# A two-layer FFT-filter and dense kernel: filter rows of two groups fetched earlier, and one piece of an inverse transform moved behind the first transposes

## The chip, the cores and the metric

One core of one Trainium2 chip. The metric is device microseconds (us) of one execution. The kernel before takes 1016.25 us (median of three runs, 1016.15 to 1018.78). Engines: PE is the matmul engine (PEld its weight loads), DVE the vector engine, ACT the activation engine, POOL the general engine, which here mostly issues DMAs, and SP a queue that issues DMAs.

## The reference, cut to what matters

```python
def _A_ref(x, w_r, w_i):                       # spectral layer, x is 1 x 2048 x 1024 bf16
    X = rfft2(x.astype(float32), axes=(-2, -1))
    X = X * (w_r + 1j * w_i)                   # filter, 2048 x 513
    return irfft2(X, s=(S, D), axes=(-2, -1)).astype(bfloat16)

def _B_ref(x, w1, b1, w2):                     # dense layer, 1024 -> 3584 -> 1024
    h = einsum("bsd,df->bsf", x, w1) + b1
    ...                                        # act = Mish(h)
    return einsum("bsf,fd->bsd", act, w2)

x = A_x
x = x + _A_ref(_layernorm(x), A_w_r, A_w_i)
x = x + _B_ref(_layernorm(x), B_w1, B_b1, B_w2)
x = x + _A_ref(_layernorm(x), A_w_r, A_w_i)
x = x + _B_ref(_layernorm(x), B_w1, B_b1, B_w2)
```

## The kernel before

The FFTs are products with DFT matrices on PE. A spectral layer first transforms all of the input with one set of matrices (the first step; in the first layer these are scaled matrices, the tile MN). The rest is cut into 8 groups of frequencies. Each group goes through a second step, a filter multiplication, a third step and two inverse steps, and its result goes through memory (`u_scratch`) into a buffer `UT`. When all 8 are there, the last inverse step (`i4`) makes the output. The groups overlap in a fixed order; in the code `stage, g, h` are the step, the group and its half.

In the first layer the filter must be put into the order of the groups. Its rows come from memory into a ring of two buffers (`WR`), four small matmuls (`filter_bins`) and three engines of copies turn them into filter tiles:

```python
def load_w(self, g):
    if self.li == 0:
        self.load_wr(self.WR[g % 2], g)        # two DMAs: real rows, imaginary rows
        return
    ...

self.s1(li)                                    # first step, frees MN
...
self.UT = self.alloc("UT", o["UT"], [P, P])    # lies over MN
...
for stage, g, h in self.order_A():
    if stage == 2:
        s2(g, h)
        if li == 0 and h == 0:
            filter_bins(g)
            if g < 6:
                load_w(g + 2)                  # waits until the copies of g have read WR
    elif stage == 3:
        s3(g, h)
        if h:
            if g < 6:
                load_tabs(g + 2)               # forward table
            ...
    elif stage == 4:
        i1(g, h)
        if h and g < 6:
            load_btabs(g + 2)                  # inverse table, tile name c_bt
    else:
        i2(g, h)
        u_turn(g, h)
```

All these loads stand in POOL's one queue, in program order (in the trace of before, group 6's two row transfers at 67.45 and 68.16, the table after them at 68.89).

The dense layer starts (its "head") with what the spectral layer left to do for the first rows: `i4` for four blocks of rows, then the layer norm of the first two, their transposes on PE, and the first dense matmuls. The other 12 blocks of rows of `i4` are cut into pieces, called by `rest(bank)`, that are strewn among the first dense matmuls:

```python
        self.root(0, 2)
        rest(0)                                # 15 matmuls of 96 columns, one wide ACT evacuation
        rest(3)                                # 15 more, the piece that the change moves
        for j in range(2):
            xn[j] = self.apply(j)              # DVE: normalise
        for j in range(2):
            transposed(0, j, xn[j])            # PE: 8 transposes each, DVE copies them out
        self.warm(ACT.Mish)                    # ACT: table load
        at_tiles(0)
        ...
        for fg in range(4):
            mm1(0, fg, 0, ...)                 # first dense matmuls
            rest(3)
```

## Time and profile before

The profiled execution spans 1013.1 us. Of the page, besides what the prediction shows, the chain of work that ended last (the first line by engine, the second by line of code; each figure is a share of the span) is what tells how little can be reached here:

```profile
PE 87%; DMA 4%; SPq 3%; DVE 2%; ACT 2%; issue 1%; POOL 0%; ACTq 0%; DVEq 0%
PE PS L1067 38%; PE PS L1050 38%; SPq L249 3%; PE PS L771 2%; PE PS L697 2%; PE PS L792 2%; PE PS L961 2%; DMA ARENA<-in_A_w_i_dram 1%; DMA ARENA<-u_scratch 1%; DMA ARENA<-c_bt 1%; DMA u_scratch<-ARENA 1%; PE PS L1016 1%; PE PS L743 1%; ACT ARENA L778 1%; PE PS L810 1%
```

L1050 and L1067 are the two dense products. The waits on `in_A_w_i_dram` (filter rows) and on `c_bt` are 1% each, some 10 us each with their whole flight times.

### The profile page before, as it was taken

To read this page: it belongs to the slowest core of one execution; us is meant where nothing else is said; L and a number is where in the kernel's file an instruction comes from. 1 tells how busy PE (TensorE), PEld (TensorE's weight loads), DVE (VectorE), ACT (ScalarE), POOL (GpSimd) and SP (SyncE) were. 2 spreads that over 40 slices of the span, in tenths; PEclk is the share of its full clock that TensorE was granted. 3 is DMA by queue.
4 is the path that set the end of the run, shared out by engine and by line. 5 is a ranking of instruction groups with operands and counts; after the bars stand their busy time and mean duration, and the time that the engine had idled before them with its cause. 6 is when DMAs were issued, how large, how long until landed. Compare 5 with 4: busy or idle time off the path is not lost.

```text
span 1013.1 us, 13670 instructions
## 1 busy us (share of the span) xinstructions
PE 952.0 (94%) x5749; PEld 506.0 (50%) x5833; DVE 323.9 (32%) x673; ACT 348.7 (34%) x484; POOL 81.6 (8%) x114
## 2 busy tenths in 40 slices
PE   1799799999999999999999978999999999999998
PEld 0576575444444444444456747644444444444443
DVE  7797468002443000033347736830011100000111
ACT  7898474340000343300029848533100023430000
POOL 4651000000000000002421100000000000000000
PEclk9999899999999999999999999999999999999999
DMA  9979813652110220002922875256411212100000
GB/s 284 248 231 321 217 47 115 204 194 61 47 47 30 76 81 21 1 21 90 196 58 83 233 188 156 75 163 201 129 25 45 74 52 83 42 1 11 21 28 25
DMA packets 154205, 107.00 MB, mean 106 GB/s; under 512 B 74448, under 2 KB 133664, under 8 KB 154144
## 3 DMA queue, kind: packets, MB, share of 16 engines
q1 hardware_dynamic: 143056, 78.61, 27.4%
q0 software_dynamic: 8912, 25.84, 8.8%
q10 hardware_dynamic: 2176, 1.66, 0.5%
q8 instruction: 47, 0.77, 0.3%
q14 instruction: 14, 0.11, 0.0%
HBM read 80.85 MB, written 20.71 MB: 100 GB/s over the span
## 4 chain that ended last, share of the span: by engine, by line
PE 87%; DMA 4%; SPq 3%; DVE 2%; ACT 2%; issue 1%; POOL 0%; ACTq 0%; DVEq 0%
PE PS L1067 38%; PE PS L1050 38%; SPq L249 3%; PE PS L771 2%; PE PS L697 2%; PE PS L792 2%; PE PS L961 2%; DMA ARENA<-in_A_w_i_dram 1%; DMA ARENA<-u_scratch 1%; DMA ARENA<-c_bt 1%; DMA u_scratch<-ARENA 1%; PE PS L1016 1%; PE PS L743 1%; ACT ARENA L778 1%; PE PS L810 1%
## 5 line engine op out<-in xcount | busy, mean ns | idle before, releaser
L1050 PE MATMUL PS<-ARENA 128*128 128x512 bf16 (+1 forms) x1950 | 389.1, 358 | 3.8 <-DVE ARENA L1021 1.9
L1067 PE MATMUL PS<-ARENA 128*128 128x512 bf16 x1756 | 385.5, 379 | 1.9
L1054 ACT ACTIVATE ARENA<-PS,B 128x512 bf16<-128x512 f32 (+1 forms) x248 | 159.4, 645 | 412.1 <-PE PS L1050 411.6
L1050 PEld LDWEIGHTS PS<-ARENA 128*128 128x128 bf16 x1984 | 193.0, 98 | 194.7 <-DVE ARENA L1021 2.9
L1067 PEld LDWEIGHTS PS<-ARENA 128*128 128x128 bf16 x1792 | 175.3, 98 | 211.4
L1072 DVE TENSOR_TENSOR XS<-PS,XS 128x512 bf16<-128x512 f32 x64 | 44.3, 692 | 586.9 <-PE PS L1067 586.9
L460 DVE BATCH_NORM_STATS2 BN<-XS 128x6 f32<-128x512 bf16 x100 | 64.6, 674 | 5.4 <-DMA XS<-in_A_x_dram 4.3
L249 POOL DMA_DIRECT2D xn_scratch<-ARENA x12 | 6.5, 541 | 374.2 <-DVE ARENA L512 374.2
L771 PE MATMUL PS<-ARENA 128*128 128x256 bf16 x256 | 32.4, 273 | 4.0 <-DVE ARENA L760 3.2
L778 ACT ACTIVATE ARENA<-PS 128x1024 bf16<-128x1024 f32 x32 | 33.1, 1054 | 6.8 <-PE PS L771 6.8
L432 ACT ACTIVATE RS<-MV,EPS 128x2 f32<-128x2 f32 (+2 forms) x5 | 1.5, 297 | 96.8 <-DVE MV L463 96.2
L697 PE MATMUL PS<-FD,ARENA 128*128 128x256 bf16 (+1 forms) x256 | 31.8, 271 | 2.4 <-ACT ARENA L617 1.2
L749 ACT ACTIVATE ARENA<-PS 128x1024 bf16<-128x1024 f32 x32 | 32.5, 1044 | 4.5 <-PE PS L745 4.5
L771 PEld LDWEIGHTS PS<-ARENA 128*128 128x128 bf16 x256 | 24.2, 98 | 11.8 <-DVE ARENA L760 5.5
L753 DVE TENSOR_TENSOR ARENA<-ARENA 128x1024 bf16<-128x1024 bf16 x32 | 22.0, 688 | 20.4 <-ACT ARENA L749 20.2
L961 PE MATMUL PS<-MT,ARENA 128*128 128x32 bf16 (+1 forms) x512 | 21.4, 199 | 7.1 <-DMA ARENA<-u_scratch 3.8
L697 PEld LDWEIGHTS PS<-FD,ARENA 128*128 128x128 bf16 x256 | 24.4, 98 | 6.5 <-DVE ARENA L619 1.4
L820 ACT ACTIVATE ARENA<-PS 128x1024 bf16<-128x1024 f32 x26 | 26.8, 1066 | 2.4 <-PE PS L792 2.4
L792 PE MATMUL PS<-ARENA,BD 128*128 128x256 bf16 x192 | 24.9, 273 | 2.3 <-ACT ARENA L778 2.3
L512 DVE TENSOR_SCALAR ARENA<-XS,MV,RS 128x1024 bf16<-128x1024 bf16 x48 | 25.0, 545 | 1.0
L961 PEld LDWEIGHTS PS<-MT,ARENA 128*128 128x128 bf16 x512 | 20.0, 102 | 9.8 <-issue 4.5
L732 ACT ACTIVATE ARENA<-PS 128x1024 bf16<-128x1024 f32 x22 | 22.9, 1058 | 3.1 <-PE PS L697 3.1
(79 smaller groups left out, 516.5 us busy)
## 6 DMA issues: line engine op xcount, KB each, us to landing
ARENA<-in_B_w_dram SPq DMA_DIRECT2D x56, 512.0 KB, 3.9
ARENA<-in_B_w_dram SPq DMA_DIRECT2D x56, 256.0 KB, 4.2
u_scratch<-ARENA SPq DMA_DIRECT2D x14, 512.0 KB, 4.4
ARENA<-u_scratch SPq DMA_DIRECT2D x14, 512.0 KB, 6.1
w_scratch<-ARENA POOLq DMA_DIRECT2D x8, 512.0 KB, 5.8
ARENA<-w_scratch POOLq DMA_DIRECT2D x8, 512.0 KB, 5.2
out_dram<-XS SPq DMA_DIRECT2D x16, 256.0 KB, 2.1
ARENA<-xn_scratch POOLq DMA_DIRECT2D x15, 256.0 KB, 10.6
```

The source lines that it names most:

```text
L249: return eng.dma_start(out_ap, in_ap).then_inc(ds.sem, 16)
L460: self.op(self.dve, lambda e: e.bn_stats(self.BN[:, j, 6 * h:6 * h + 6], self.XS[:, j, 512 * h:512 * h + 512]), reads=[self.r_xs[j]], part ...
L697: fns.append(lambda e: e.matmul(dst, at(r), FD[:, t:t + n], start=start, stop=stop))
L749: self.op(act, lambda e: e.activation(x.ap.rearrange("p a b -> p (a b)"), ps, ACT.Copy, scale=SIG), reads=banks, writes=[x.res])
L771: fns.append(lambda e, c=c, part=part: e.matmul(ps[:, c * 256:(c + 1) * 256], yk.ap[:, part, c * P:(c + 1) * P], t[:, (128, 0)[part]:(384, ...
L778: self.op(act, lambda e: e.activation(v.ap[:, :, i, :], src, ACT.Copy), reads=banks, parts=[v.res])
L792: fns.append(lambda e, dst=dst, part=part, c=c: e.matmul(dst, BD[:, c:c + P], mov(kd, part), start=(part == 0), stop=(part == 1)))
L961: fns.append(lambda e, l=l: e.matmul(self.PS[:, bank + l // k, l % k * w:(l % k + 1) * w], self.UT.ap[:, u0 + l, :], self.MT[:, 8 * lo:8 * ...
L1050: fns.append(lambda e, db=db, bank=bank, fl=fl: e.matmul(PS[:, bank, 0:w], wb.ap[:, db, fl * P:(fl + 1) * P], x.ap[:, db, tok], start=(db ...
L1054: self.op(act, lambda e, bank=bank, ft=ft: e.activation(at.ap[:, ft, tok], PS[:, bank, 0:w], ACT.Mish, bias=self.B1[:, ft:ft + 1]), reads= ...
L1067: fns.append(lambda e, i=i, ft=ft: e.matmul(PS[:, bank, :], at.ap[:, ft, t * P:(t + 1) * P], W2[ft].ap[:, h * 512:(h + 1) * 512], start=(i ...
L1072: self.op(dve, lambda e: e.tensor_tensor(xs, PS[:, bank, :], xs, ALU.add), reads=[self.r_bank[bank]], writes=[self.r_xs[j]])
```

## The change

Two parts. Rows: `UT` isn't needed until the first group comes back from memory, so its space, which MN leaves after the first step, serves as two more row buffers (`WX`) for groups 2 and 3. Rows of groups 2 to 5 can then be fetched earlier, and PE should no longer wait for those of group 2. Piece: the second `rest(3)` goes behind the first transposes, into the time in which PE waits for DVE to copy them out.

```diff
+    def wr(self, g):
+        return self.WX[g - 2] if g in (2, 3) else self.WR[g % 2]
     def load_w(self, g):
         if self.li == 0:
-            self.load_wr(self.WR[g % 2], g)
+            self.load_wr(self.wr(g), g)
...                                              (filter_bins uses wr(g) too)
+        def open_ut():                         # UT is opened at the first read-back
+            self.UT = self.alloc("UT", o["UT"], [P, P])
...
-        self.UT = self.alloc("UT", o["UT"], [P, P])
...
+        self.UT = None
+        if li == 0:
+            self.WX = [self.alloc(f"WX{i}", o["UT"] + 4096 * i, [2, 2, 512]) for i in range(2)]
+            for g in (2, 3):
+                load_w(g)
         for stage, g, h in self.order_A():
...
                     filter_bins(g)
-                    if g < 6:
+                    if g in (0, 1):
+                        load_w(g + 4)
+                    elif g in (4, 5):
                         load_w(g + 2)
...
         rest(0)
-        rest(3)
         for j in range(2):
             xn[j] = self.apply(j)
         for j in range(2):
             transposed(0, j, xn[j])
         self.warm(ACT.Mish)
+        rest(3)
```

The change shifts line numbers: L697 becomes L701, L922 L937, L933 L948, L771 L775, L961 L976, L1016 L1031 and L1050 L1065.

## The prediction

> **What bounds the kernel now.** I read the page first: where PE stands, and which engines share the first spectral stage.
>
> ```profile
> PE 952.0 (94%) x5749; PEld 506.0 (50%) x5833; DVE 323.9 (32%) x673; ACT 348.7 (34%) x484; POOL 81.6 (8%) x114
> ```
>
> PE is busy for 952.0 of 1013.1 us, and the chain that ended last is 38% and 38% the two big matmul groups of the dense layers. The change touches neither. All that it can reach lies in the other 61.1 us in which PE is idle, and in the small groups between. So I went to PE's timeline of the first spectral layer (28 to 112 us) and looked for idle time that the change can remove. Two waits there are for data:
>
> ```profile
> 47.29 0.62 PE L922 MATMUL PS<-ARENA 128*128 128x256 bf16 x4 [1.10 <-DMA ARENA<-in_A_w_i_dram]
> ...
> 78.19 1.03 PE L771 MATMUL PS<-ARENA 128*128 128x256 bf16 x8 [0.85 <-DMA ARENA<-c_bt]
> ```
>
> The first is the filter matmuls of group 2: PE stood 1.10 us until the second half of that group's filter rows landed. The second is the inverse step of group 4, 0.85 us for its table. POOL's timeline says when those transfers were issued:
>
> ```profile
> 40.77 0.76 POOL L249 DMA_DIRECT2D ARENA<-in_A_w_r_dram  x1 [3.96 <-DVE ARENA L933]
> 41.53 0.73 POOL L249 DMA_DIRECT2D ARENA<-in_A_w_i_dram  x1
> ...
> 67.45 0.71 POOL L249 DMA_DIRECT2D ARENA<-in_A_w_r_dram  x1 [7.01 <-PE PS L697]
> 68.16 0.73 POOL L249 DMA_DIRECT2D ARENA<-in_A_w_i_dram  x1
> 68.89 0.91 POOL L249 DMA_DIRECT2D ARENA<-c_bt  x1
> ```
>
> Group 2's rows went out only at 40.77, when group 0's filter matmuls (39.59 to 40.2 on PE) had released the two-deep ring. The table behind the 0.85 us left at 68.89 behind group 6's rows, which had waited for DVE's filter copies of group 4 (L933, 65.77 to 67.16), and landed 9.17 us later in the chain.
>
> A PE wait is worth its length only if no other engine is full there. ACT's timeline, where each start-to-start step of a full evacuation back to back is 0.90 us:
>
> ```profile
> 45.81 1.12 ACT L749 ACTIVATE ARENA<-PS 128x1024 bf16<-128x1024 f32 x1
> 46.71 1.13 ACT L732 ACTIVATE ARENA<-PS 128x1024 bf16<-128x1024 f32 x1
> 47.94 0.87 ACT L937 ACTIVATE ARENA<-PS 128x384 bf16<-128x384 f32 x2
> 48.81 1.02 ACT L749 ACTIVATE ARENA<-PS 128x1024 bf16<-128x1024 f32 x1
> ...
> 56.80 1.13 ACT L820 ACTIVATE ARENA<-PS 128x1024 bf16<-128x1024 f32 x1
> 57.96 1.02 ACT L749 ACTIVATE ARENA<-PS 128x1024 bf16<-128x1024 f32 x1
> ```
>
> ACT hardly felt PE's 1.10 us: 46.71 to 47.94 is 1.23, so 0.33 was lost, and 0.87 instead of the 0.74 that such a pair takes elsewhere is 0.13 more. By stretches of 5 us ACT is busy 4.90, 5.00, 4.97, 5.00, 5.00 from 43 to 68 us, and DVE 4.90, 4.80, 4.55, 4.73 from 48 to 68. Three engines are in balance there.
>
> The other place is the head of each dense layer, where the last inverse step (L961) runs beside the first transposes (L1016). First layer, then second:
>
> ```profile
> 119.02 2.58 PE L961 MATMUL PS<-MT,ARENA 128*128 128x96 bf16 x30 [1.67 <-ACT XS L550]
> 119.98 1.00 DVE L512 TENSOR_SCALAR ARENA<-XS,MV,RS 128x1024 bf16<-128x1024 bf16 x2
> 121.40 1.40 PE L1016 MATMUL PS<-IDENT,ARENA 128*128 128x128 bf16 x16
> ...
> 611.28 1.45 PE L961 MATMUL PS<-MT,ARENA 128*128 128x96 bf16 x30 [1.67 <-ACT XS L550]
> 612.84 1.08 PE L1016 MATMUL PS<-IDENT,ARENA 128*128 128x128 bf16 x16
> ```
>
> The 30 matmuls of L961 are the two pieces of 15; the change moves the second one. In the first layer they take 86 ns each and PE reaches the transposes after DVE has made their input (120.98). In the second they take 48 ns and the transposes start right when DVE delivers (612.24 plus 0.54 is 612.78). The granted clock explains it: 0.50 in every half microsecond from 115.5 to 122.0, but 1.00 from 610.5 on. In both layers PE then sits 0.94 and 0.93 us until DVE has copied the transposes (L1021), before the first dense matmul at 123.74 and 614.85.
>
> [...] the dips run from about 115.1 to 122.1 (two windows) and 606.75 to 610.2 (one). [...] the DMA share of 1.0 and more from 37 to 43 us is the constants of SP's queue[...]. [...]
>
> **The change part by part.** Nothing is removed or added: POOL still issues the same 12 row transfers, PE the same matmuls.
>
> Part A, rows. The rows of groups 2 and 3 go into space that the last scaled first-step matmul frees (L611, ends about 37.6), instead of waiting for group 0 and 1. With POOL's half microsecond of reaction they go out at about 38.1 instead of 40.77: 2.6 us earlier. Even with a landing 1 us slower than the 5.63 us seen, for the constants beside it, group 2 is there at 45.5; PE wants it at 47.29 - 1.10 = 46.2. So the 1.10 us wait goes. Groups 4 and 5 go out by 44 instead of 50.88 and 56.29, so the tables behind them leave earlier too; nothing waited for those.
>
> How much of 1.10 survives? ACT gets 0.33 + 0.13 = 0.46 at 48 us, and 0.25 at 57.96 (56.80 to 57.96 is 1.16, less 0.90). DVE is the tighter one: it runs unbroken from 45.19 and lets go only about 0.1 at 52.6 and 0.2 at 56.1, and 0.42 at 61.77 which follows ACT. PE needs the bank that DVE evacuates at 58.13 to 59.35 for its matmuls at 59.50, so PE can be only 0.3 to 0.4 early there. About 0.5 then reaches DVE's filter copies of group 4 at 65.77, by that the issue of group 6's rows and of the table at 68.89, and by that the wait at 78.19, whose landing sets everything after it. That wait stays, perhaps longer (PE arrives earlier than the table). Part A: -0.5 us, between 0 and -1.1.
>
> Part B, first dense layer. One piece of 15 at 86 ns is 1.29, so PE is free at 120.3; DVE's first input is ready at 119.98 + 0.54 = 120.52; eight slow transposes (0.70) to 121.2, a copy of 0.65, the second copy to about 122.6. PE needs 2.58 + 1.40 in all from 119.02, plus 0.2 idle, some of it now at full clock, so it is ready at about 123.0 against 123.74: -0.75. ACT: first piece out to about 121.8, table load to 123.3, second piece out to 124.7, then the first Mish; PE's next piece wants those banks at about 124.75. It just fits.
> Second dense layer. The transposes wait for DVE at 612.78 already, so they cannot start earlier; the moved 15 matmuls (0.7 us) fit into the 0.93 us gap. ACT's first Mish moves from 616.27 to about 616.4. Gain 0, perhaps 0.1 lost.
> The 0.75 exists only when the slow clock falls on this spot[...]; I give it two chances in three: -0.5.
>
> Sum: 1016.25 - 0.5 - 0.5 = 1015.2; I say 1015.1.
>
> **The rivals.** (1) The whole 1.10 us arrives, because PE runs ahead and ACT's later idle steps (66.86 to 68.22, 69.15 to 70.42) are squeezed out too, and both dense layers gain: about -2.2, 1014.0. For it: PE is named in the chain from 47.29 to 67.4. Against: the table wait at 78.19 stands behind DVE, not PE. (2) The wait is only traded: the table at 78.19 lands when it did, since the transfers around it (store and read-back of the first group, from 67.11 and 67.47) are what slows it, 9.17 against a median of 6.1 us. Then part A is 0 and the time 1015.7. (3) Four groups of rows at once, 2 MB from 38 us in the busiest DMA stretch, delay group 2's forward table (issued 44.19, wanted about 53): at some 290 GB/s they need until about 46 to 50, so this is close but hidden; if not, +0.5 to +1. (4) PE is less dense in the clock window at 118.6 to 122, with one gap more, and the slow clock holds one window longer: +1 to +3 us, some 1 in 15.
>
> **Range and chances.** The mechanism is worth 0 to 2.2 us. The runs of before lie from 1014.96 (profiled) to 1018.78, so the noise is as large; 1013.4 to 1016.9 holds both. Two per cent is 20 us, more than everything touched can give: within 2% almost surely.
>
> **What would show it.** Right: POOL issues four row transfers in a block at 38 to 41; PE has no wait at the third L922 group; ACT has no step of 1.23 around 47; the table wait before L771 near 78 is still there and not shorter; in the first dense layer L961 comes as 15, then L1016, then 15, with L1050 starting up to 0.8 earlier after ACT's last L550 of the residual; in the second the distance is unchanged. Wrong: PE waiting for the forward table (L742) near 53, group 2's rows landing after 46.2, the table wait gone, or a dense head with the slow clock reaching into L1050.

1016.25 - 0.5 - 0.5 is 1015.25, written as 1015.2, and the forecast was 1015.1. The trace of before shows: the granted clock is 0.50 from 115.30 to 122.12 and from 606.82 to 610.23; POOL was idle for 5.57 us before group 4's row transfers at 50.88, and the table and the store behind them followed at 52.34 and 52.90; ACT's table load takes 1.28 us (at 123.17). The two chances in three for the slow clock, and the 1 us that the constants' transfers might cost the rows, are estimates.

## More of the kernel before

To compare traces I cut each into stretches at fixed instructions of PE, by the start of that instruction's first weight load. These stretches of the kernel before will be used throughout (us):

| stretch | first layers | second layers |
|---|---|---|
| start to the first matmul of the second step ("start") | 38.69 | |
| from there to the first half of group 4's first inverse step ("to the table") | 39.48 | 33.90 |
| from there to the last first-inverse-step matmul | 23.94 | 23.50 |
| to the first matmul of `i4` | 10.17 | 12.67 |
| to the first `apply` on DVE | 7.71 | 6.54 |
| `apply` to the first dense matmul ("head") | 3.76 | 2.60 |
| the first 96 dense matmuls, with the pieces among them ("first 96") | 16.18 | 16.18 |
| the rest of the dense layer (in the first column with the next layer's first step, up to its second) | 395.71 | 382.04 |

"To the table" holds both waits that the rows can touch; "head" and "first 96" hold the moved piece.

## The result, and the profile after

| | runs | median us | lowest to highest |
|---|---|---|---|
| before | 4 | 1016.2 | 1014.7 to 1018.78 |
| after | 4 | 1016.61 | 1016.38 to 1017.72 |

The ratio is 1.0004, with a 95% interval of 0.9982 to 1.0025. Ratios and intervals here are formed from the runs of the same rounds; they are not quite the ratio of the medians, nor always that of the plain means. All outputs are right. The time is the same. In the profiled executions the changed kernel is even longer, 1014.9 us against 1013.1 (span).

The page of the changed kernel, in the line that answers to the first one of the prediction:

```profile
PE 962.4 (95%) x5833; PEld 509.9 (50%) x5833; DVE 323.7 (32%) x673; ACT 348.7 (34%) x484; POOL 82.1 (8%) x114
```

PE looks 10 us busier, but this is no work: the trace of before lacks 84 matmul records (5749 of 5833, while its weight loads are complete). One has to see such a gap before reading the busy sum (the prediction's 61.1 us of idle time is some 10 us too much for this reason); the stretches above use weight loads for this reason.

**The rows did what they were meant to do.** POOL's timeline after (start, length, engine, line, operation, tiles, then in brackets the idle time before it and what ended it):

```profile
39.19 0.86 POOL L249 DMA_DIRECT2D ARENA<-in_A_w_r_dram  x1 [1.05 <-PE PS L611]
40.05 1.29 POOL L249 DMA_DIRECT2D ARENA<-in_A_w_i_dram  x1
...
44.95 0.73 POOL L249 DMA_DIRECT2D ARENA<-in_A_w_i_dram  x1
```

Eight row transfers leave in one block, released by the last scaled matmul (L611). Group 2's second half landed 6.78 us after its issue, at 46.83. The same part of PE's timeline:

```profile
47.51 0.61 PE L937 MATMUL PS<-ARENA 128*128 128x256 bf16 x4
...
60.58 0.39 PE L746 MATMUL PS<-ARENA 128*128 128x512 bf16 x1 [0.45 <-DVE ARENA L738]
...
76.05 0.62 PE L937 MATMUL PS<-ARENA 128*128 128x256 bf16 x4 [0.24 <-DMA ARENA<-in_A_w_i_dram]
...
79.40 1.03 PE L775 MATMUL PS<-ARENA 128*128 128x256 bf16 x8 [0.77 <-DMA ARENA<-c_bt]
```

At 47.51 the third filter group starts without a wait; before it had stood 1.10 us. But PE, now early, stands 0.45 us at 60.58 for a bank that DVE empties, another 0.24 at 76.05 for group 6's rows, and still 0.77 at 79.40 for the table. "To the table" is 39.21 us against 39.48. The chain of waits of the changed kernel says what that last wait hangs on (start, length, what):

```profile
68.49 1.29 POOL ARENA L249 x2
...
69.92 9.34 DMA ARENA<-c_bt
...
79.40 1.03 PE PS L775 x8
```

The table flies for 9.34 us, and it was issued behind the two row transfers of group 6 (POOL, 68.49 to 69.78 and on), as before.

**The heads.** PE in the first dense head of the changed kernel, then in the second:

```profile
119.71 1.38 PE L976 MATMUL PS<-MT,ARENA 128*128 128x96 bf16 x15 [1.67 <-ACT XS L550]
121.26 1.89 PE L1031 MATMUL PS<-IDENT,ARENA 128*128 128x128 bf16 x16 [0.17 <-DVE ARENA L512]
122.94 1.41 PE L976 MATMUL PS<-MT,ARENA 128*128 128x96 bf16 x15
124.15 2.73 PE L1065 MATMUL PS<-ARENA 128*128 128x256 bf16 x16
...
611.97 0.81 PE L976 MATMUL PS<-MT,ARENA 128*128 128x96 bf16 x15 [1.67 <-ACT XS L550]
613.53 1.55 PE L1031 MATMUL PS<-IDENT,ARENA 128*128 128x128 bf16 x16 [0.75 <-DVE ARENA L512]
614.87 1.41 PE L976 MATMUL PS<-MT,ARENA 128*128 128x96 bf16 x15
616.08 2.53 PE L1065 MATMUL PS<-ARENA 128*128 128x256 bf16 x16
```

The piece of 15 is where it was put, and PE's idle stretch of 0.93 us before the first dense matmul is gone in both. In the first head the way from the first piece to the dense matmuls is 4.44 us (119.71 to 124.15) against 4.72 before. But the first 16 dense matmuls take 2.73 us and 2.53 us: PE starts them at a granted clock of 0.50 (from 119.00 to 125.82, and from 613.93 to 617.34). Before, it was granted 1.00 there in both heads, and they took 1.92. In these two traces every recorded stretch of half or full clock, but for the last, which the end cuts, is a whole multiple of 3.41 us long (3.41, 6.83, 85.3 to 484.7); 3.41 us is called a window here. Two windows around the second head, one line each (start:end, length, then for each engine busy time and count of instructions, PEclk the granted clock, DMA share, GB/s), before:

```profile
610.23:613.64 3.41, 2.25 (x44) 2.10 (x45) 2.99 (x9) 3.20 (x7) 0.00 (x0) 1.00 1.12 332
613.64:617.05 3.41, 2.48 (x32) 2.12 (x30) 3.38 (x7) 3.30 (x5) 0.00 (x0) 1.00 1.01 274
```

and after:

```profile
610.52:613.93 3.41, 1.22 (x23) 1.07 (x23) 3.20 (x10) 3.20 (x6) 0.00 (x0) 1.00 1.14 339
613.93:617.34 3.41, 3.41 (x33) 3.05 (x31) 2.88 (x6) 2.77 (x4) 0.00 (x0) 0.50 1.19 303
```

Before, PE was busy for 2.25 of the 3.41 us of the first window and kept the full clock. After, one piece less stood ahead of the transposes and the window fell a little differently; PE was busy for 1.22, and the next window was granted at half. (Busy time alone does not tell which it will be: in the changed kernel PE was busy for 2.46 us of the window from 115.58, and the next one was at half. The last section has what does better.)

**Where the 1.8 us between the two profiled executions come from**, by the stretches: the start is 1.47 longer (40.16 against 38.69; the last scaled matmuls, after which the early row loads are issued, already begin 1.33 later, at 38.28 against 36.95, so this is hardly the loads' doing), the first spectral layer to its last first-inverse-step matmul 0.27 shorter, from there to the end of the first 96 dense matmuls 0.01 longer (37.83 against 37.82), the rest up to the second layer's second step 0.08 longer, and the same stretch of the second head 0.57 longer (38.56 against 37.99; its head and first 96 alone 1.17 longer). The sum is 1.86.

### The profile page after: what moved, and what is told of

Its sections match the earlier page's. It is cut to its first block, busy times and chain, and to the rows that moved or that the text cites. A ratio compares the mean times of both kernels' runs of the same rounds, so it can differ in the third digit from the quotient of the medians.

```text
span 1014.9 us, 13752 instructions
## 1 busy us (share of the span) xinstructions
PE 962.4 (95%) x5833; PEld 509.9 (50%) x5833; DVE 323.7 (32%) x673; ACT 348.7 (34%) x484; POOL 82.1 (8%) x114
## 3 DMA queue, kind: packets, MB, share of 16 engines
q1 hardware_dynamic: 143056, 78.61, 27.3%
## 4 chain that ended last, share of the span: by engine, by line
PE 87%; DVE 4%; DMA 3%; ACT 2%; SPq 2%; issue 0%; ACTq 0%; POOL 0%; DVEq 0%
PE PS L1082 38%; PE PS L1065 38%; PE PS L775 2%; SPq L249 2%; PE PS L701 2%; PE PS L976 2%; PE PS L796 2%; DMA ARENA<-c_bt 1%; DMA ARENA<-in_A_x_dram 1%; PE PS L1031 1%; DMA ARENA<-u_scratch 1%; DVE ARENA L619 1%; DMA u_scratch<-ARENA 1%; PE PS L611 1%; ACT ARENA L782 1%; PE PS L814 1%
## 5 line engine op out<-in xcount | busy, mean ns | idle before, releaser
L1065 PE MATMUL PS<-ARENA 128*128 128x512 bf16 (+1 forms) x1984 | 392.3, 359 | 0.1
L1065 PEld LDWEIGHTS PS<-ARENA 128*128 128x128 bf16 x1984 | 193.8, 98 | 193.2 <-DVE ARENA L1036 0.7
L782 ACT ACTIVATE ARENA<-PS 128x1024 bf16<-128x1024 f32 x32 | 33.9, 1080 | 7.0 <-PE PS L775 7.0
L775 PE MATMUL PS<-ARENA 128*128 128x256 bf16 x256 | 32.4, 273 | 4.0 <-DVE ARENA L764 3.2
L753 ACT ACTIVATE ARENA<-PS 128x1024 bf16<-128x1024 f32 x32 | 33.3, 1071 | 4.5 <-PE PS L749 4.5
L701 PE MATMUL PS<-FD,ARENA 128*128 128x256 bf16 (+1 forms) x256 | 31.8, 271 | 2.5 <-DVE ARENA L948 1.3
L775 PEld LDWEIGHTS PS<-ARENA 128*128 128x128 bf16 x256 | 24.0, 98 | 12.1 <-DVE ARENA L764 5.7
L824 ACT ACTIVATE ARENA<-PS 128x1024 bf16<-128x1024 f32 x26 | 27.4, 1087 | 2.4 <-PE PS L796 2.4
L976 PE MATMUL PS<-MT,ARENA 128*128 128x32 bf16 (+1 forms) x512 | 22.3, 200 | 5.9 <-ACT XS L550 3.3
L701 PEld LDWEIGHTS PS<-FD,ARENA 128*128 128x128 bf16 x256 | 24.4, 98 | 6.6 <-DVE ARENA L948 1.4
L976 PEld LDWEIGHTS PS<-MT,ARENA 128*128 128x128 bf16 x512 | 20.7, 102 | 8.7 <-ACT XS L550 3.5
L736 ACT ACTIVATE ARENA<-PS 128x1024 bf16<-128x1024 f32 x22 | 23.3, 1075 | 3.2 <-PE PS L701 3.2
```

Of the source, the lines that this page charges most:

```text
L701: fns.append(lambda e: e.matmul(dst, at(r), FD[:, t:t + n], start=start, stop=stop))
L753: self.op(act, lambda e: e.activation(x.ap.rearrange("p a b -> p (a b)"), ps, ACT.Copy, scale=SIG), reads=banks, writes=[x.res])
L775: fns.append(lambda e, c=c, part=part: e.matmul(ps[:, c * 256:(c + 1) * 256], yk.ap[:, part, c * P:(c + 1) * P], t[:, (128, 0)[part]:(384, ...
L782: self.op(act, lambda e: e.activation(v.ap[:, :, i, :], src, ACT.Copy), reads=banks, parts=[v.res])
L824: self.op(act, lambda e: e.activation(dst, ps, ACT.Copy), reads=banks, parts=[u.res])
L976: fns.append(lambda e, l=l: e.matmul(self.PS[:, bank + l // k, l % k * w:(l % k + 1) * w], self.UT.ap[:, u0 + l, :], self.MT[:, 8 * lo:8 * ...
```

## The experiments

The theory: each part does its local work, but both are worth little, the rows 0.3 to 0.5 us because the table wait and DVE's work follow, the piece nothing at full clock and a little at half, which the clock takes back. The rivals: the rows are worth the whole 1.10 us and the loss is elsewhere; the table wait simply swallows the rows, so that they are worth nothing; the piece costs time in itself. Twelve runs were made. Their main stretches, with those of the two kernels, are here (us; the times and ratios follow with each run):

| run | start | to the table | head 1 | first 96 | head 2 | first 96 | span |
|---|---|---|---|---|---|---|---|
| before | 38.69 | 39.48 | 3.76 | 16.18 | 2.60 | 16.18 | 1013.07 |
| after | 40.16 | 39.21 | 3.41 | 17.07 | 3.08 | 16.87 | 1014.91 |
| same_again | 39.02 | 39.71 | 3.27 | 18.05 | 3.76 | 16.18 | 1016.45 |
| change_again | 39.43 | 39.11 | 3.41 | 17.74 | 3.41 | 17.03 | 1017.17 |
| rows_only | 39.87 | 39.17 | 3.97 | 16.18 | 3.86 | 16.18 | 1014.85 |
| piece_only | 39.76 | 39.39 | 3.27 | 16.18 | 3.27 | 16.18 | 1013.16 |
| table_only | 39.68 | 38.75 | 3.55 | 16.18 | 3.45 | 16.19 | 1014.36 |
| rows_and_table | 40.53 | 38.04 | 3.45 | 16.18 | 3.66 | 16.18 | 1014.76 |
| kept_warm | 45.15 | 37.81 | 2.60 | 16.19 | 4.10 | 16.18 | 1034.64 |
| kept_warm_piece | 49.21 | 37.79 | 4.09 | 16.18 | 2.73 | 16.19 | 1038.55 |
| arena_moved | 44.37 | 43.28 | 2.60 | 16.18 | 2.60 | 16.18 | 1035.96 |
| kept_warm2 | 38.64 | 38.11 | 4.09 | 16.18 | 3.95 | 16.18 | 1014.55 |
| kept_warm2_piece | 40.05 | 38.02 | 2.60 | 16.26 | 3.23 | 16.49 | 1014.32 |
| kept_warm2_again | 40.83 | 38.46 | 4.03 | 16.18 | 2.60 | 16.18 | 1015.88 |

### The two parts apart: same_again, change_again, rows_only, piece_only

These four ran in the same rounds, beside 11 runs of the kernel before (median 1017.78 us, 1015.02 to 1022.17).

same_again is the kernel before, unedited, for the noise.

> The kernel before, run against itself: it measures the noise that every other run here stands in. Both theories: ratio 1.000 within 0.1%. If the trace's start (the first spectral matmul at 38.72 us in the trace of before, 40.19 in the changed one) differs from 38.72 by over half a microsecond here too, the 1.5 us that the changed kernel's trace showed there is the start of the run and not the change.

Measured: 1016.93 us, ratio 0.9994 (0.9974 to 1.0014). Its start is 39.02, only 0.33 later than in before; that the start alone can move by more is shown by piece_only and table_only (39.76 and 39.68), whose code is the same up to there.

change_again is the changed kernel, unedited.

> The change once more. My theory: the spectral stage is 0.3 to 0.5 us shorter from its first matmul to the table wait, and the dense heads lose or win up to 1.2 us each by where the slow clock falls, so the sum is within 1 us of before, ratio 0.9990 to 1.0010. Rival (all waits removed arrive): ratio 0.998, -2 us. Rival (the prefetch overloads the transfers): group 2's forward table is waited for, +0.5 us or more in the spectral stage.

Measured: 1016.25 us, ratio 0.9983 (0.9961 to 1.0005): outside the 0.9990 to 1.0010 expected, but with 1 in its interval.

rows_only is the changed kernel with the piece put back:

```diff
         rest(0)
+        rest(3)
         for j in range(2):
             xn[j] = self.apply(j)
...
         self.warm(ACT.Mish)
-        rest(3)
```

> Only the rows of groups 2 and 3 earlier; the dense heads as before. My theory: no wait at the third filter group (1.10 us in before), the table wait near 78 us still 0.7 to 0.9 us, and from the first spectral matmul to the inverse step after that wait 39.2 us instead of 39.47: -0.3 to -0.5 us in all. Rival (whole wait arrives): 38.4, -1.1 us. Rival (transfers set it): 39.4 or more, no gain.

Measured: 1016.64 us, ratio 0.9993 (0.9973 to 1.0014).

piece_only is the kernel before with the piece moved:

```diff
         rest(0)
-        rest(3)
...
         self.warm(ACT.Mish)
+        rest(3)
```

> Only the second piece of the last inverse step behind the first transposes; the rows as before. My theory: with the clock full, first dense matmul no earlier in either layer (the transposes wait for VectorE's input); with the clock at half in the first head 0.6 to 0.8 us earlier; and in one or both heads the slow clock comes back within the transposes or the first dense matmuls (0.50 granted beyond the transposes), which costs 0.5 to 1.2 us. Sum 0 to +1.2 us. Rival (no clock effect, the gap is simply filled): -0.7 us in the first layer, 0 in the second.

Measured: 1016.45 us, ratio 0.9995 (0.9972 to 1.0017). The expected return of the slow clock did not come in either head, and both heads take 3.27 us at half clock, 0.4 less than the mean of those without the piece (3.64), not 0.6 to 0.8.

What follows. By whole times, no part can be told from nothing: each interval holds 1, and the kernel before against itself gives 0.9994. The stretches repeat far better. "To the table" is 39.48, 39.71 and 39.39 without the rows and 39.21, 39.11 and 39.17 with them: means 39.53 and 39.16, so the rows are worth 0.36 us (of the unrounded means). Neither the whole 1.10 us nor nothing fits. The noise of the whole time sits in the start, which runs from 38.64 to 40.83 among the kernels whose addresses are those of before, and in the heads, where half-clock windows fall differently.

In the heads of piece_only the dense matmuls are not slowed, although the same piece was moved. Its windows, the one with the first piece and the transposes and the one after it, first head:

```profile
119.43:122.84 3.41, 3.23 (x34) 3.02 (x35) 2.58 (x7) 2.61 (x4) 0.00 (x0) 0.50 1.19 295
122.84:126.25 3.41, 3.31 (x49) 2.97 (x47) 3.27 (x7) 3.05 (x5) 0.00 (x0) 1.00 1.15 302
```

Here the window begins exactly with the first piece (119.43), PE is busy for 3.23 of 3.41 us, and the next window is at full clock. In the changed kernel the window from 119.00 to 122.41 held part of a wait, PE was busy for 2.53, and the clock stayed at half (0.50) for another window. So moving the piece need not slow the dense matmuls; the two windows lie differently, 0.00 and 0.71 us ahead of the first piece.

### The table instead of the rows: table_only, rows_and_table

If the table wait is the one that the whole stretch hangs on, issuing that table ahead of group 6's rows should give more than the rows did, without touching them. These two and the next two ran beside 11 runs of the kernel before (median 1017.58 us). table_only, on the kernel before:

```diff
                     filter_bins(g)
-                    if g < 6:
+                    if g < 6 and g != 4:
                         load_w(g + 2)
...
                 if h and g < 6:
                     load_btabs(g + 2)
+                if li == 0 and (g, h) == (2, 1):
+                    load_w(6)
```

> The kernel before, with one order changed on the issuing queue: the inverse table of group 4 goes out ahead of group 6's filter rows instead of behind them. If the table wait near 78 us is what sets the end of the first spectral stage, that wait (0.85 us) goes and the distance from the first spectral matmul to the inverse step of group 4 falls from 39.5 us (39.48, 39.71 and 39.39 in three traces) to 38.7, though the filter wait of 1.10 us stays. If the busy evacuation engines set it, the distance stays within 0.2 of 39.5.

Measured: 1016.24 us, ratio 0.9987 (0.9973 to 1.0002). "To the table" is 38.75, 0.78 us less than the mean of before. The wait is gone; PE's timeline of table_only has the second half of group 3's inverse step and the first of group 4's in one run of 16:

```profile
77.65 1.92 PE L771 MATMUL PS<-ARENA 128*128 128x256 bf16 x16
```

rows_and_table is rows_only with the same edit (the row load of group 6 moved out of `elif g in (4, 5)`).

> The change's row part and the table's new order together, dense heads as before. If the two waits are in series, as I hold, the gains add: 39.16 (rows alone) less 0.8 is about 38.3 to 38.5 us[...]. If the rows' gain and the table's gain are the same slack seen twice, it is 38.7, as with the table alone.

Measured: 1016.59 us, ratio 0.9990 (0.9977 to 1.0004). "To the table" is 38.04: 1.49 us less than before, and less than the 38.3 to 38.5 expected. The two alone give 0.36 and 0.78, together 1.14, so the rows are worth more (0.71) once the table no longer stands behind them. That is what two waits in series would give: removing the first mostly moves the time into waits further on, and only both together let it through. There is one trace of each of these two kernels, but five later ones with both edits repeat the larger gain (37.79 to 38.46). The spans (1014.36 and 1014.76) still do not show it, since the start (39.68 and 40.53 against 38.69) and the half-clock windows of these executions (granted clock 0.993 and 0.992 in the mean against 0.995) eat it.

### Keeping the clock up: kept_warm, kept_warm_piece, and an address

The windows that half clock followed were, in the traces of before and after, among the ones with the fewest columns streamed by PE (last section). If part B is lost to the clock, then, so the conjecture, useless matmuls in PE's idle stretches keep it at full and make the heads comparable. kept_warm is rows_and_table with these:

```diff
+            self.ZT = sb("ZT", [64])                     # a tile of zeros, 128 bytes of each partition
...
+    def add_zeros(self, n, bank):
+        self.group([lambda e: e.matmul(self.PS[0:64, bank, :], self.ZT[:], self.FD[:, 0:512], start=False, stop=False)] * n, ...)
...
+                if g == 7:
+                    self.spin((3, 4)[h], 2 * (self.npair % 4))      # useless matmuls before the last inverse steps
...
+                if (g, h) == (7, 0):
+                    self.spin(4, 2 * (self.npair % 4))
...
-        self.spin(8, 0)
+        self.spin(15, 2 * (self.npair % 4))
...
+        self.add_zeros((5, 9)[li], 7)                    # before i4
         for u in range(4):
+            if u == 1 and li == 0:
+                self.add_zeros(2, 7)
...
+        self.spin(2, 0)
         rest(0)
```

> As rows_and_table, with matmuls of no use (overwritten, or adding zeros) in TensorE's waits of the spectral tail and the first part of each dense head[...]; dense heads in the order of before. If the slow windows are TensorE's low activity, fewer or no windows at 0.50 appear between 98 and 125 us and between 598 and 620, the heads take about 19.8 us (as the one undisturbed head of before) instead of 20.9 to 22.3, and the run is 2 to 4 us under before. If matmuls of zeros do not count as activity or the windows have another cause, the windows stay and it gains only the 1.1 us of the spectral stage or loses some tenths for the added matmuls.

Measured: 1035.63 us, ratio 1.0169 (1.0145 to 1.0192).

kept_warm_piece is the same with the piece moved and `spin(2, 6)` ahead of the transposes.

> As kept_warm, with the change's second part (second piece behind the first transposes). With the clock full throughout, my theory says that the head is as long as without it, 19.8 us, since the transposes wait for VectorE's input either way. If filling the gap is worth something at full clock, 19.1 to 19.4. If the slow clock returns in a head, that head doesn't count.

Measured: 1035.76 us, ratio 1.0179 (1.0156 to 1.0202).

Both are 18 us slower, and not mainly where the useless matmuls stand: the start is 6 to 10 us longer, and the rest up to the second layer's second step, which has none of them, 6.4 us (402.24 and 402.10 against 395.71). All of that 6.4 lies after the last dense matmul, where PE waits 6.3 us in kept_warm for a transfer from ARENA to ARENA (1.8 before). "To the table" was the shortest yet (37.81 and 37.79). One side effect of the edit was the new tile of zeros: it is allocated ahead of the large tile ARENA and moves it by 128 bytes. So the next call tried that alone, and the useless matmuls without it. It ran beside 9 runs of the kernel before (median 1017.21 us).

arena_moved is the kernel before with an unused tile 128 bytes longer:

```diff
-            sb("PAD1", [32])
+            sb("PAD1", [96])
```

> The kernel before with 128 bytes of padding more ahead of its big arena, and nothing else: it asks whether the 18 us of kept_warm are the address alone. If so: 1030 to 1036 us, first spectral matmul at 43 us or later, 78 to 79 us from there to the last inverse step. If not: 1016 to 1018.

Measured: 1036.67 us (two runs), ratio 1.0189 (1.0170 to 1.0207). The address alone costs it. ARENA lies 128 bytes further in each partition than before. The page's part on DMA issues (last column: us from issue to landing), before:

```profile
ARENA<-in_B_w_dram SPq DMA_DIRECT2D x56, 256.0 KB, 4.2
u_scratch<-ARENA SPq DMA_DIRECT2D x14, 512.0 KB, 4.4
ARENA<-u_scratch SPq DMA_DIRECT2D x14, 512.0 KB, 6.1
```

and in arena_moved:

```profile
ARENA<-in_B_w_dram SPq DMA_DIRECT2D x56, 256.0 KB, 4.3
u_scratch<-ARENA SPq DMA_DIRECT2D x14, 512.0 KB, 5.8
ARENA<-u_scratch SPq DMA_DIRECT2D x14, 512.0 KB, 8.1
```

The read-backs of `u_scratch`, which write rows of 256 bytes into ARENA, take a third longer (8.1 against 6.1 us); the loads of the second dense weights, which write rows of 2048 bytes into ARENA, do not (4.3 against 4.2). The stores have rows of 4096 bytes. Their median is longer too (5.8 against 4.4); whether by their own address or by the read-backs beside them was not isolated. Over the whole trace the 143056 packets of queue q1, as many as before, took 29.6% of 16 engines' span of 1036.0 us against 27.4% of 1013.1, which is some 34.3 ns a packet against 31.0 (an estimate from these shares).

Why the address costs this was not shown: no run isolated it, and other offsets were not tried.

One more thing is in this trace. From the first spectral matmul to `i4` arena_moved takes 85.6 us, not the 78 to 79 expected: it has the late rows and the late table of the kernel before, and PE now waits 2.43 us for the rows of group 2 and 1.67 at the table, so that "to the table" is 43.28 (in one stretch of it PE was slow too: the eight matmuls from 55.92 take 1.91 us, like ones elsewhere 1.04). kept_warm, at the same shifted address but with both fetched earlier, has neither wait and 37.81. In this pair the early fetches were worth more; the transfers were slower (in arena_moved the imaginary rows on POOL's queue took 6.5 us in the median against 5.3 before, the inverse tables 6.4 against 6.1), which is a likely reason.

### The clock again, with no address moved: kept_warm2, kept_warm2_piece, kept_warm2_again

kept_warm2 is kept_warm with the zeros in a pad that was there already:

```diff
-            sb("PAD0", [64])
+            self.ZT = sb("PAD0", [64])
...
-            self.ZT = sb("ZT", [64])
```

> kept_warm again, with the tile of zeros in bytes that were padding, so that every other buffer stays at its address. If the 18 us of kept_warm were the moved addresses[...], the stages are back to 75 us from the first spectral matmul to the last inverse step (78.8 there), and the run is 1 to 4 us under before by the clock windows saved. If the added matmuls themselves cost it, it stays at 1030 or more.

Measured: 1015.27 us (1013.95 to 1016.35), ratio 0.9975 (0.9961 to 0.9988). The 18 us are gone, which confirms the address from the other side.

kept_warm2_piece moves the piece in that kernel:

```diff
         rest(0)
-        rest(3)
...
         self.warm(ACT.Mish)
+        rest(3)
```

> kept_warm2 with the second part of the change and nothing in the gap before the transposes. With a full clock in a head: from VectorE's first input to the fifth pair of dense matmuls 18.8 us, as the undisturbed heads without the part had (18.78, 18.79), so the part is worth 0 to 0.1 there. If filling the gap pays at a full clock: 18.1. With the half clock at the head: 19.4 where it ends by the first dense matmul, 20 and more where it doesn't.

Measured: 1016.14 us, ratio 0.9985 (0.9973 to 0.9998). Its first head ran at full clock, with the piece moved (15 matmuls of 128x96 take 0.80 us; in the changed kernel, at a granted 0.50, 1.38 and 1.41):

```profile
121.10 0.80 PE L989 MATMUL PS<-MT,ARENA 128*128 128x96 bf16 x15
122.40 1.08 PE L1044 MATMUL PS<-IDENT,ARENA 128*128 128x128 bf16 x16 [0.49 <-DVE ARENA L514]
123.31 0.80 PE L989 MATMUL PS<-MT,ARENA 128*128 128x96 bf16 x15
124.40 1.92 PE L1078 MATMUL PS<-ARENA 128*128 128x256 bf16 x16 [0.29 <-DVE ARENA L1049]
```

PE waits 0.49 us for DVE's first input and 0.29 for DVE's copies: at full clock DVE sets the pace of this head, whether the piece is there or not. From `apply` to the first dense matmul it takes 2.60 us, to the hundredth what five full-clock heads without the moved piece take (before, second layers; kept_warm, first; arena_moved, both; kept_warm2_again, second). So at full clock the piece is worth 0.00 up to the first dense matmul (kept_warm_piece's second head, with two useless matmuls ahead of its transposes, has 2.73). After it the piece can cost something: the first 96 of the two heads, all at full clock, take 16.26 and 16.49 against 16.18 (which piece_only has too). The next piece starts when ACT has emptied the moved one, which had to stand behind the table load: at 126.23 after 126.17, and at 617.85 after 617.80, 0.07 and 0.30 later after the first dense matmul than the usual 1.76.

kept_warm2_again repeats the best version in new rounds, on another chip (11 runs of before, median 1017.28 us).

> kept_warm2 once more, on another chip or at another time, since it is the only version whose interval (0.9961 to 0.9988) lay clear of before. If its gain is real (1.5 us of the first spectral stage, and fewer slow windows), the ratio is 0.996 to 0.999 again and the distance from the first spectral matmul to the inverse step of group 4 is 38.0 to 38.2 us. If it was luck with the clock's phase, the ratio is 0.9990 to 1.0005.

Measured: 1015.95 us (1013.97 to 1017.69), ratio 0.9974 (0.9957 to 0.9992). "To the table" was 38.46 here, longer than in the other runs with both edits (37.79 to 38.11): PE stood 0.50 us at the filter matmuls of group 6 for ACT, not for a transfer.

What follows. kept_warm2 is 0.25% faster than the kernel before, twice, with both intervals below 1. The changed kernel wasn't in its rounds; against before it gave 1.0004 and 0.9983, both intervals holding 1, so kept_warm2 is the only one of these that is shown to beat the kernel before by repeated rounds (kept_warm2_piece, 0.9985, did so in one set). Of its 2.0 to 2.5 us, 1.1 to 1.4 lie in "to the table", less 0.3 in each spectral layer for the useless matmuls (24.23 against 23.94, and 23.78 against 23.50). The rest should be fewer half-clock windows. There are fewer for all runs: the mean granted clock was 0.9984 and 0.9983 against 0.9927 and 0.9935 of before in the same rounds, and one window of 3.41 us at half takes 0.0017 off it (half of 3.41 in some 1015), so some three windows fewer (an estimate). What they are worth was not measured.

## Why the prediction was right or wrong

The time (1015.1 predicted, range 1013.4 to 1016.9; 1016.61 measured) and "within 2%" held. The range also held the time of no change at all (1016.25), so that it held says little. The gain of 1.15 us did not show (the sum of the parts, 1015.25, had been lowered to 1015.1 without a reason); here are its steps.

**Part A, "-0.5 us, between 0 and -1.1": right.** The rows gave 0.36 us over three traces with and three without (0.27 in the profiled pair). The mechanism was also the one named. The 1.10 us wait went in every trace with the rows. PE was stopped by the bank that DVE empties, for 0.45 us at 60.58. Counted from the first matmul of the second step this is 20.42 us against 20.81 before: 0.39 early, where the prediction had 0.3 to 0.4. ACT has no step of 1.23 left. The table wait "is still there": 0.77 against 0.85. It said "not shorter", and that was a little off: it is 0.77 in after, 0.76 in change_again and 0.46 in rows_only. The rows of group 2 landed 6.8 us after issue, where "1 us slower than the 5.63" had been allowed; they were still 0.7 us early (46.83 is later than the 46.2 that the prediction named as a sign of being wrong, but this execution's start was 1.47 us later).

**Rivals (1), (2), (3).** The whole 1.10 us did not arrive (1), the wait was not merely traded (2), and PE never waited for the forward table (3). What the prediction did not see is how cheaply the wait behind it all could be removed: it named the table's issue behind group 6's rows, yet only table_only showed that this order, and not the rows, held 0.78 us, and 1.49 with the rows.

**Part B, first dense layer, "-0.75" when the slow clock falls on it, times two chances in three: the step that failed.** The term had two errors. Its size: over the half-clock heads of the runs at the old addresses and without useless matmuls, the way from `apply` to the first dense matmul is 3.64 us without the moved piece (mean of nine heads) and 3.31 with it (six heads, one of which turned slow midway), so 0.33 us are saved, not 0.75. The prediction took part of the moved work at full clock, since in the trace of before the slow windows ended at 122.1; in the changed trace they ended only at 125.8, and all of 15 matmuls, 16 transposes and 15 matmuls ran at half clock (granted 0.50; 4.44 us in place of 4.72). And it stopped counting at the first dense matmul. The first 96 are longer in four of the six heads with the piece (16.87 to 17.74 against 16.18), but in only one of the ten without it (18.05, in same_again). Head and first 96 together have a mean of 20.15 us with the piece and 19.90 without (ten heads, the one at full clock among them): nothing is left of the gain. Also "it just fits", said of ACT, failed where the clock was full: in kept_warm2_piece the second piece's evacuation held the next one up by 0.07 and 0.30 us.

**Second dense layer, "gain 0, perhaps 0.1 lost": right in the one head that was at full clock throughout** (2.60 with and without, then 16.26 against 16.18; a first-layer head), but the changed kernel did not stay at full clock there: 3.08 plus 16.87 in place of 2.60 plus 16.18, 1.17 us.

**Rival (4), "the slow clock holds one window longer", was given 1 in 15.** In the profiled run of the changed kernel it is what happened, in both heads (head and first 96 +0.54 and +1.17): the prediction's own sign of being wrong, "a dense head with the slow clock reaching into L1050". That the moved piece makes it likelier is suggested by four heads in six against one in ten. In the second head the matmuls of the window from 610.52 streamed some 1960 columns; the moved piece has 1440, and with them there it would have been some 3400 (an estimate), more than in any window that half clock followed in the two traces that the last section counts (some 3010 at most). But where the windows lie differs from run to run (the first head's last half-clock window began at 118.71 in before, at 122.41 in after, 0.31 us before the first piece and 2.70 after it), piece_only escaped it in both heads, and the granted clock of all runs does not show it: its mean is 0.9934 in 16 runs of after, change_again and piece_only and 0.9932 in 66 with the piece in its old place (before, same_again, rows_only, table_only, rows_and_table), where one more window in every run would be 0.0017. So in one head the moved piece plausibly made the difference; that it does so on average is not shown.

**"The noise is as large": right, and more so than thought.** The start alone moves by 2.2 us (38.64 to 40.83).

## What to carry to other kernels

When a wait is removed, look for the next wait behind it in the chain and ask what that one hangs on; here swapping two issues in one queue was worth twice the new buffers (0.78 against 0.36 us), and both together seemed worth more than their sum (1.49 against 1.14). Where the granted clock changes beside a change, as here in steps of 3.41 us, count to the end of the half-clock window, not to the end of the wait that the change fills. And compare stretches between fixed instructions when whole times scatter by more than the effect; watch the addresses too, since here an edit that adds 128 bytes ahead of a DMA buffer buried what was being measured (1036.67 against 1017.21 us).

## What the traces show of the clock and of the moved address

- Half clock came without a long gap: it followed a window in which PE's longest gap was 1.67 us (after, 610.52). PE's busy time in a window does not tell which clock follows: 2.46 of 3.41 us was followed by half (after, 115.58), 1.58 by full (after, 101.93). The columns that the matmuls stream in a window do better (a matmul of 128x96 counts 96, a transpose 128; each is placed by the end of its record), whether the window itself is at half or full clock. In the traces of before and after, up to the end of PE's work, the 7 windows that half clock followed had at most some 3010 columns (after, 115.58), and the other 568 at least some 2900 (after, 101.93). So the two ranges touch. This is a count from two traces; the ends of matmuls are modelled, and the trace of before lacks 84 of their records.
- In piece_only's window from 119.43 PE ran the 15 matmuls of the first piece (1440 columns) and 16 transposes (2048 columns, 120.99 to 122.67, about half of the window), and the next window was granted 1.00. The 1440 alone are fewer than in any window that full clock followed in the two traces counted above (an estimate from these counts). So here the transposes seem to have counted.
- 128 bytes of address cost 1036.67 against 1017.21 us in arena_moved, with the read-backs that write 256-byte rows slowed from 6.1 to 8.1 us. Why was not shown.
